# Six spare matmuls in front of the first five products of the second stage of a spectral mixer

## The chip, the cores and the metric

The kernel runs on one core of a Trainium2 chip. The metric is the device time of one execution in microseconds; the median of several executions is compared. A profiled execution gives the trace that is read here.

## The reference

The input `x` has 2048 tokens of 512 channels. It is normalised over the channels, and two branches work on the result: a two-dimensional Fourier filter, and a two-layer network over the token axis, whose output gates the filter's.

```python
xn = _layernorm(x, axis=-1)
# A: filter in the frequency domain
X = rfft2(xn, axes=(-2, -1)) * (w_r + 1j * w_i)
s = irfft2(X, s=(S, D), axes=(-2, -1))
# B: token mixing, W1 is 2048 x 1792, W2 is 1792 x 2048
h = _layernorm(xn, axis=-1)
u = gelu(einsum("bsd,sf->bdf", h, w1) + b1)
y = einsum("bdf,fs->bds", u, w2) + b2
return x + s * silu(y.transpose(0, 2, 1))
```

## The kernel before

Tokens stand on the 128 partitions, 16 of them to a partition, so that there are 16 blocks of 128 tokens by 512 channels. Matrix products that need float32 accuracy are made of three products of operands in the rounded float32 type (`F32R`): high by high, high by low, low by high, where a high part is a copy by ScalarE and a low part a subtraction by VectorE.

The first stage multiplies `w1` with the normalised tokens, in matmuls of 512 columns, and works the forward Fourier transform and the filter in between them. Its last four partial sums are `last_sum` (L759). The results `u` go through GELU and become the moving operands `fa`, `fb`, `fc` and `fd` of the second stage.

The second stage (from L799) works on pairs of token blocks, `p` and `p + 8`, for `p` from 0 to 7. Each pair takes seven products instead of eight, by sums of blocks of `w2` in the manner of Strassen; `ORDER` (L801) is the order of the seven, by their numbers: 1, 2, 5, 6, 3, 7, 4. By the names of their moving operands that is `fd`, `fa`, `fc`, `fc`, `fa`, `fb`, `fb`. The weights of a product are a tile `w2f` with a high and a low half of seven 128x128 blocks each; `w2_forms` (L843) makes them ahead of time, the high half on ScalarE, the low half on VectorE. A product is 21 matmuls of 256 columns, three passes over the seven blocks: the low half is read in the third pass. It accumulates in bank 2 or 3, 4 or 5 of PSUM (`banks`, L903; `products`, L906).

Before the last product of pairs 0 to 6 TensorE works a block of small float32 matmuls, the inverse Fourier transform of the pair (`PARTS`, L44: in pair 0 the even channels, 64x64 matmuls, and the odd ones, 128x128; in pair 1 odd, even and the part over tokens, `spectral`, of 64x512; in pairs 2 to 6 even, `spectral`, odd). In pair 7 `spectral` and `channels` (eight calls of 128x128) stand before the fifth product and a last `spectral` before the seventh. These blocks write banks 6 and 7 of PSUM.

The order on each engine is the order of the program here: an object `Kept` (L131) records every operation as it is called, so that most lines of the trace are L139, the line of that helper. `T` is TensorE, `A` ScalarE, `V` VectorE, `G` GpSimd, `SY` the SyncE queue. A matmul call is a weight load (LDWEIGHTS, engine name PEld) and a matmul (MATMUL, engine name PE) in the trace; the type float32 takes two of each.

`cft` is a float32 constant of 128x130 that is loaded in the first stage (L522).

Of the kernel before, what the change touches and what calls it, by code (L numbers as in the profile page):

```python
# [16 lines left out]
P = 128  # L17
# [124 lines left out]
def spectral_mixer_kernel(tc, x, w1, b1, w2, b2, wk, we, wx, c_f, c_ft, c_d, c_i, c_g, c_h, out):  # L142
    nc = tc.nc
    V, A, G, T, SY = nc.vector, nc.scalar, nc.gpsimd, nc.tensor, nc.sync
# [17 lines left out]
    with tc.tile_pool(name="ps", bufs=1, space=PSUM) as psp, ExitStack() as left, ExitStack() as right:  # L162
        ps = psp.tile([P, 8, 512], F32, name="ps")
        pers = pool(left, "left", "pers", 1)
        cf = pers.tile([P, 64], F32, name="cf")
        cft = pers.tile([P, P + 2], F32, name="cft")
# [158 lines left out]
        def w1_tiles(j):  # L325
            return [[w1r.tile([P, NE1 * P], F32R, name=f"w1{n}{a}_{j}", tag=f"w1{n}{a}", bufs=3) for n in "hl"] for a in range(2)]
# [94 lines left out]
        def form_parts(n, i):  # L421
            t, k = form[i][n]
            return t[:, k, :D // 2], t[:, k, D // 2:]
# [38 lines left out]
        T = Kept(T, keep)  # L462
# [22 lines left out]
        w = w1_tiles(0)  # L485
# [23 lines left out]
        for j in range(NJ):  # L509
# [25 lines left out]
            start, more_stats = j < 3, j + 3 < NJ  # L535
            if more:
                w = w1_tiles(j + 1)
# [248 lines left out]
        for n in range(8):  # L786
            a, b, c, d, e, f = PACE[n]
            u, v, w = ([None] * (k < MADE[n]) for k in range(3))
# [12 lines left out]
        ORDER = (1, 2, 5, 6, 3, 7, 4)  # L801
# [101 lines left out]
        def banks(p):  # L903
            return ps[:, 2 + p % 2, :HD], ps[:, 4, :HD], ps[:, 5, :HD]

        def products(p, n):  # L906

            wf = ready.pop(0)
            bx, by, bz = banks(p)
            o = {1: bx, 6: bx, 7: bx, 4: bx, 2: by, 5: bz, 3: bz}[n]  # L910

            for a, (wi, ui) in enumerate(((0, 0), (0, 1), (1, 0))):
                for m, i in enumerate(FORMS):
                    T.matmul(o, wf[:, wi, i], form_parts(n, i)[ui], start=m + a == 0 and n in (1, 2, 5),
                             stop=m == NH - 1 and a == 2, skip_group_check=n in (6, 3, 7, 4))

        def copied(name, src, where):
            t = where.tile([P, HD], F32, name=name, tag=name.split("_")[0], bufs=1)
            step(A.activation(t, src, AF.Copy))
            return t  # L920

        products(0, ORDER[0])
        p1 = copied("p1_0", banks(0)[0], w2p)
        next(wforms)
# [4 lines left out]
        rest_b = form_b_high(5), form_b_high(6)  # L929
        step(A.activation(e1[:1, 0, :1], b1t[:1, :1], AF.Silu))  # L930
        products(0, ORDER[1])
        next(wforms)
        low_part(rest_b[0])
# [118 lines left out]
        for p in range(NP):  # L1052
# [8 lines left out]
            for k, n in enumerate(ORDER):  # L1061
                started = not p and k < 2
                if not started:
                    products(p, n)
# [81 lines left out]
```

## Time and profile before

| what | value |
| --- | --- |
| median of 3 executions | 365.92 us (365.81 to 365.93) |
| profiled execution | 365.86 us |
| its span, from first to last instruction | 364.1 us |
| TensorE matmuls busy | 357.3 us (98%) |
| TensorE weight loads busy | 308.1 us (85%) |
| VectorE busy | 305.6 us (84%) |
| ScalarE busy | 211.1 us (58%) |
| GpSimd busy | 87.2 us (24%) |

Busy times are those of one profiled execution. Matmuls are pipelined and their printed durations overlap; what a matmul takes in a row of them is read from the distance of starts. In a timeline, neighbours of the same names are one row, with their count behind an x.

### The profile page before, as it was taken

Reading aid. Unit: us, or ns where it says so; the run is one execution under the profiler, and the core shown is the slowest. Engines: PE = TensorE matmul, PEld = TensorE weight load, DVE = VectorE, ACT = ScalarE, POOL = GpSimd, SP = SyncE. Lnnn points to the kernel's source line nnn. Section 1 sums busy time; section 2 is a strip of 40 time slices with the busy share of each in tenths; the row PEclk is TensorE's granted clock in tenths of the full one; section 3 lists DMA queues with packets and bytes.
Section 4 is the critical chain, followed back from the end, with each engine's and each line's share of the span. In section 5 each row is a group of like instructions: output and inputs, shape, how many; then the busy total and the mean of one; then the engine's idle time right before and its main releaser. Section 6 shows DMA issues by size and latency. Waiting matters only on the chain.

```text
span 364.1 us, 8781 instructions
## 1 busy us (share of the span) xinstructions
PE 357.3 (98%) x3444; PEld 308.1 (85%) x3444; DVE 305.6 (84%) x587; ACT 211.1 (58%) x385; POOL 87.2 (24%) x134
## 2 busy tenths in 40 slices
PE   7999999999999999999999999999999999999994
PEld 4788888888877778777888999989898989898983
DVE  5899999967799995999996988687887969696984
ACT  4887788867534426755227875555464546565441
POOL 4233333323222012220120001050403123140330
PEclk9999999999999999999999999999999999999999
DMA  7978899406595686976568388698888989898724
GB/s 208 251 185 200 202 265 311 190 2 164 173 254 193 189 252 165 260 243 200 167 221 181 101 227 180 184 175 204 186 188 209 178 219 167 228 161 220 122 27 90
DMA packets 33293, 68.66 MB, mean 189 GB/s; under 512 B 4612, under 2 KB 19380, under 8 KB 33124
## 3 DMA queue, kind: packets, MB, share of 16 engines
q1 hardware_dynamic: 24276, 42.44, 41.3%
q0 software_dynamic: 8496, 25.01, 32.0%
q10 hardware_dynamic: 480, 0.66, 0.6%
q8 instruction: 27, 0.44, 0.5%
q14 instruction: 14, 0.11, 0.1%
HBM read 59.70 MB, written 8.13 MB: 186 GB/s over the span
## 4 chain that ended last, share of the span: by engine, by line
PE 97%; DMA 1%; ACT 0%; DVE 0%; ACTq 0%; issue 0%; DVEq 0%
PE ps L139 97%; DMA w1r<-in_w_dram 1%; DVE rows L139 0%; ACTq L453 0%; ACT w1h L467 0%; ACT g L139 0%; DVEq L1142 0%
## 5 line engine op out<-in xcount | busy, mean ns | idle before, releaser
L139 PE MATMUL ps<-h,w1h 128*128 128x512 f32 x400 | 116.3, 397 | 0.0
L139 PEld LDWEIGHTS ps<-h,w1h 128*128 128x128 f32 x400 | 72.9, 188 | 19.8 <-issue 4.9
L139 PE MATMUL ps<-h,w1l 128*128 128x512 f32 x200 | 67.6, 390 | 0.0
L139 DVE TENSOR_TENSOR w2f<-a,w2f 128x896 fp32r<-128x896 f32 x36 | 39.2, 1089 | 21.2 <-ACT w2f L139 21.2
L139 ACT ACTIVATE w2f<-a 128x896 fp32r<-128x896 f32 x36 | 36.9, 1025 | 12.9 <-PE ps L139 8.0
L139 PEld LDWEIGHTS ps<-h,w1l 128*128 128x128 f32 x200 | 37.5, 188 | 8.1
L139 PE MATMUL ps<-fb,w2f 128*128 128x256 f32 x336 | 41.9, 279 | 0.0
L139 PE MATMUL ps<-fa,w2f 128*128 128x256 f32 x336 | 41.3, 278 | 0.0
L139 POOL DMA_DIRECT2D s<-in_w_dram x14 | 18.4, 1311 | 95.8 <-DMA s<-in_w_dram 59.8
L139 PEld LDWEIGHTS ps<-fb,w2f 128*128 128x128 f32 x336 | 39.7, 188 | 1.6 <-ACT g L139 0.8
L139 PE MATMUL ps<-fc,w2f 128*128 128x256 f32 x336 | 39.9, 277 | 0.0
L139 PEld LDWEIGHTS ps<-fa,w2f 128*128 128x128 f32 x336 | 39.8, 188 | 0.0
L139 PEld LDWEIGHTS ps<-fc,w2f 128*128 128x128 f32 x336 | 39.2, 188 | 0.0
L155 ACT ACTIVATE w1h<-w1s 128x512 fp32r<-128x512 f32 x26 | 16.2, 632 | 27.0 <-DMA w1s<-in_w_dram 14.7
L139 POOL DMA_DIRECT2D out_dram<-r x28 | 23.6, 1278 | 27.4 <-DVE r L139 27.4
L668 POOL DMA_DIRECT2D xc<-xc x16 | 9.8, 620 | 70.3 <-ACT xc L666 55.1
L308 POOL TENSOR_TENSOR ey<-t 128x256 f32<-128x256 f32 x16 | 15.7, 979 | 43.7 <-DVE t L306 43.7
L139 ACT ACTIVATE w2f<-s 128x896 fp32r<-128x896 f32 x15 | 15.3, 1020 | 14.4 <-PE ps L139 12.5
L470 DVE TENSOR_TENSOR w1l<-w1r,w1h 128x384 fp32r<-128x384 f32 x32 | 21.3, 670 | 0.0
L139 PE MATMUL ps<-fd,w2f 128*128 128x256 f32 x168 | 20.6, 277 | 0.0
L139 ACT ACTIVATE g<-c,b2t 128x256 f32<-128x256 f32 x24 | 12.1, 506 | 14.6 <-DVE c L139 14.6
L268 ACT ACTIVATE h<-x,nbm,rsm 128x256 f32<-128x256 f32 (+1 forms) x34 | 18.4, 593 | 3.7 <-DVE nbm L263 3.3
(135 smaller groups left out, 602.5 us busy)
## 6 DMA issues: line engine op xcount, KB each, us to landing
a<-in_w_dram SPq DMA_DIRECT2D x22, 448.0 KB, 4.3
wt<-in_wk_dram POOLq DMA_DIRECT2D x16, 512.0 KB, 6.2
s<-in_w_dram SPq DMA_DIRECT2D x16, 448.0 KB, 4.6
s<-in_w_dram POOLq DMA_DIRECT2D x16, 448.0 KB, 6.9
w1s<-in_w_dram SPq DMA_DIRECT2D x52, 128.0 KB, 4.4
w1r<-in_w_dram SPq DMA_DIRECT2D x28, 192.0 KB, 5.2
xc<-xc POOLq DMA_DIRECT2D x16, 256.0 KB, 3.1
out_dram<-in_x_dram SPq DMA_DIRECT2D x4, 960.0 KB, 7.4
```

What stands on the lines that cost most here:

```text
L139: return lambda *args, **kw: self.keep(operation(*args, **kw))
L155: return A.activation(hi, src, AF.Copy), V.tensor_sub(lo, src, hi.bitcast(F32))
L268: keep(A.activation(to, v, AF.Identity, bias=m["nb"][:, i], scale=m["rs"][:, i, 1:2]))
L308: G.tensor_add(ey[:, 0::3, :, j], a, b)
L470: keep(V.tensor_sub(dst, src, hi.bitcast(F32)))
L668: keep(G.dma_start(*(v.rearrange("p s t c -> p s (t c)") for v in (there[c::2], here[1 - c::2, ::-1]))))
```

## The change

`products`, which emits the 21 matmuls of one product, first calls a spare if the pair is 0 and there is one for the product's place in the order. A spare is a matmul, or two, of the given weights with the given moving operand, into the first columns of bank 6 of PSUM, where nothing reads it. `w` is the first of the product's own seven high weight blocks, 128x128, of type `F32R`; `cft` is float32. So there are, in front of the five products: one matmul of 2 columns (`F32R`), one of 2 columns (float32), one of 64 columns (`F32R`), two of 2 columns (`F32R`), one of 128 columns (float32).

```diff
@@ -906,6 +906,8 @@
         def products(p, n):
 
             wf = ready.pop(0)
+            if not p and ORDER.index(n) in spares:
+                spares[ORDER.index(n)](wf[:, 0, 0])
             bx, by, bz = banks(p)
             o = {1: bx, 6: bx, 7: bx, 4: bx, 2: by, 5: bz, 3: bz}[n]
 
@@ -913,6 +915,13 @@
+
+        def spare(lhs, rhs, times=1):
+            for _ in range(times):
+                T.matmul(ps[:, 6, :rhs.shape[1]], lhs, rhs, start=True, stop=True)
+
+        spares = {0: lambda w: spare(w, w[:, :2]), 1: lambda w: spare(cft[:, :P], cft[:, :2]), 2: lambda w: spare(w, w[:, :64]),
+                  3: lambda w: spare(w, w[:, :2], 2), 4: lambda w: spare(cft[:, :P], cft[:, :P])}
```

On TensorE, at the border of the two stages: the last matmuls of the first stage (`h`, `w1`), and the first product of pair 0 (`fd`, with the weights `w2f`). The names in brackets are the semaphores that an instruction waits for.

```order
 L139 MATMUL ps<-h_97,w1h_2557 128x512 x2
 L139 MATMUL ps<-h_97,w1l_2558 128x512
+L139 MATMUL ps<-w2f_0_2598 128x2 [waits Activation_49]
 L139 MATMUL ps<-fd_1418,w2f_0_2598 128x256 [waits Activation_49]
 L139 MATMUL ps<-fd_1418,w2f_0_2598 128x256
```

One matmul is new, with a wait of the same kind as the product behind it has; that one's own stays.

On TensorE, between the first product (`fd`) and the second (`fa`) of pair 0:

```order
 L139 MATMUL ps<-fd_2567,w2f_0_2598 128x256 x2
 L139 MATMUL ps<-fd_2656,w2f_0_2598 128x256
+L139 MATMUL ps<-cft 128x2
 L139 MATMUL ps<-fa_1456,w2f_0_2601 128x256
 L139 MATMUL ps<-fa_1563,w2f_0_2601 128x256
```

The float32 spare stands between two products whose own order is as it was. Ahead of the third product the same is done with a matmul of 64 columns, ahead of the fourth with two of 2 columns, and ahead of the fifth with a float32 one of 128 columns. The order on the other four engines is the same before and after.

## Rows read from the trace of the kernel before

**Rows 1.** The page: busy us of each engine, and the chain by engine.

```profile
PE 357.3 (98%) x3444; PEld 308.1 (85%) x3444; DVE 305.6 (84%) x587; ACT 211.1 (58%) x385; POOL 87.2 (24%) x134
...
PE 97%; DMA 1%; ACT 0%; DVE 0%; ACTq 0%; issue 0%; DVEq 0%
```

**Rows 2.** Waits of TensorE: us in total, times, longest us.

```profile
PE ps L139 <- POOL wz L443: 1.1, 1, 1.1
PE ps L139 <- ACT w1h L467: 1.1, 1, 1.1
```

**Rows 3.** Timeline of TensorE, pair 0: start us, us, what, how many.

```profile
202.54 0.39 PE L139 MATMUL ps<-h,w1l 128*128 128x512 f32 x1
202.76 2.63 PE L139 MATMUL ps<-fd,w2f 128*128 128x256 f32 x21
205.24 2.64 PE L139 MATMUL ps<-fa,w2f 128*128 128x256 f32 x21
207.71 5.11 PE L139 MATMUL ps<-fc,w2f 128*128 128x256 f32 x42
212.66 2.64 PE L139 MATMUL ps<-fa,w2f 128*128 128x256 f32 x21
215.13 2.63 PE L139 MATMUL ps<-fb,w2f 128*128 128x256 f32 x21
217.69 1.78 PE L139 MATMUL ps<-cd,yt 64*64 64x64 f32 x40
219.23 2.72 PE L139 MATMUL ps<-fb,w2f 128*128 128x256 f32 x21
221.79 2.63 PE L139 MATMUL ps<-fd,w2f 128*128 128x256 f32 x21
```

**Rows 4.** Timeline of TensorE, pair 1's last product and pair 2.

```profile
239.10 2.74 PE L139 MATMUL ps<-fb,w2f 128*128 128x256 f32 x21
241.68 2.63 PE L139 MATMUL ps<-fd,w2f 128*128 128x256 f32 x21
...
254.05 2.63 PE L139 MATMUL ps<-fb,w2f 128*128 128x256 f32 x21
```

**Rows 5.** Timeline of TensorE, from pair 2's block to pair 3's.

```profile
256.61 0.69 PE L139 MATMUL ps<-cd,yt 64*64 64x64 f32 x32
...
259.01 2.63 PE L139 MATMUL ps<-fb,w2f 128*128 128x256 f32 x21
261.48 2.54 PE L139 MATMUL ps<-fd,w2f 128*128 128x256 f32 x21
263.86 2.54 PE L139 MATMUL ps<-fa,w2f 128*128 128x256 f32 x21
...
273.38 2.54 PE L139 MATMUL ps<-fb,w2f 128*128 128x256 f32 x21
275.85 0.69 PE L139 MATMUL ps<-cd,yt 64*64 64x64 f32 x32
...
280.72 2.54 PE L139 MATMUL ps<-fd,w2f 128*128 128x256 f32 x21
```

**Rows 6.** Weight loads by stretch: stretch, length, busy (count), granted clock, DMA share, GB/s.

```profile
244.15:254.05 9.90, 9.90 (x85) 1.00 0.88 186
261.48:273.38 11.90, 11.90 (x106) 1.00 0.88 170
```

**Rows 7.** Timeline of TensorE, end of pair 7.

```profile
349.07 2.05 PE L139 MATMUL ps<-cd,yt 128*128 128x128 f32 x16
350.88 2.63 PE L139 MATMUL ps<-fa,w2f 128*128 128x256 f32 x21
353.35 2.54 PE L139 MATMUL ps<-fb,w2f 128*128 128x256 f32 x21
355.82 1.09 PE L139 MATMUL ps<-y,cft 64*64 64x512 f32 x8
356.84 2.65 PE L139 MATMUL ps<-fb,w2f 128*128 128x256 f32 x21
```

**Rows 8.** Timeline of the weight loads, pair 7.

```profile
349.07 1.86 PEld L139 LDWEIGHTS ps<-cd,yt 128*128 128x128 f32 x16 [0.81 <-ACT v L139]
350.85 1.33 PEld L139 LDWEIGHTS ps<-fa,w2f 128*128 128x128 f32 x11
```

**Rows 9.** Groups of TensorE by form: busy us, mean ns of one, idle before.

```profile
L139 PE MATMUL ps<-cf,h 64*64 64x64 f32 x512 | 9.3, 221 | 0.0
```

**Rows 10.** Timeline of ScalarE and VectorE: weights of the fifth and sixth product.

```profile
210.48 1.02 ACT L821 ACTIVATE w2f<-a 128x896 fp32r<-128x896 f32 x1 [0.26 <-DVE a L837]
...
211.53 1.09 DVE L825 TENSOR_TENSOR w2f<-a,w2f 128x896 fp32r<-128x896 f32 x1 [0.55 <-ACT w2f L821]
...
213.48 1.08 DVE L139 TENSOR_TENSOR w2f<-s,w2f 128x896 fp32r<-128x896 f32 x1
```

## The prediction

> **What bounds the kernel now.** I read the page's busy times first: TensorE's matmuls fill 357.3 of 364.1 us, no other engine more than 84% (its own weight loads, which overlap, 85%) [rows 1]. Then the chain that ended last, which is TensorE for 97% of the span [rows 1], and TensorE's waits: two, of 1.1 us each, both on the first operands of the program and over by 6.64 us [rows 2]. From there to the last product the matmuls follow one another without a hole, so every matmul that is added lengthens the span by what it takes, and every one that runs faster shortens it. ScalarE, VectorE and the queues matter only if they become late.
>
> The next view is the timeline of TensorE, since the change stands there. The second stage is eight pairs of seven products, each product 21 matmuls of 256 columns in one row of the view (42 where the third and fourth follow each other). A product's length is the distance from its start to the next product's, since the printed durations overlap. In pair 0 that is 2.48 us (202.76 to 205.24) [rows 3]; in pair 3 it is 2.38 us (261.48 to 263.86) [rows 5]. Over five products in a row: 241.68 to 254.05 is 12.37 us for 105 matmuls, 117.8 ns each [rows 4]; 261.48 to 273.38 is 11.90 us for 105, 113.3 ns each [rows 5]. So the same matmuls run at **two paces**, 2.474 and 2.380 us a product, 0.094 us apart. It is not the clock: the granted clock is 1.00, the level of 2.4 GHz, in a stretch of either pace [rows 6]. It is not a wait, as there is none. Within a run of 256-column matmuls the pace never changes; it is set where a run begins. The first run begins behind the 512-column products of the first stage and is slow at once [rows 3]. Behind it nine blocks of small matmuls (the inverse transform's 64x64, 64x512 and 128x128 ones) divide the runs. Three were entered at the slow pace: those of pair 0 and of pair 1 left it slow [rows 3, 4], that of pair 2, at 256.61, made it fast [rows 5]. Six were entered at the fast pace, those of pairs 3 to 6 and two in pair 7, and all left it fast (pair 3 and pair 7 stand in [rows 5, 7]). What in a block decides is in no row: the rows tell that the pace has a memory and that small matmuls can change it.
>
> **The change part by part.** It adds six matmul calls ahead of the first five products of pair 0, and moves nothing else: on the other four engines the order is the same, word for word but for buffer numbers. Slow are 20 products: six of pair 0 up to its block (stretch 0), then its last product and six of pair 1 (stretch 1), then the last of pair 1 and six of pair 2 (stretch 2). At the fast pace they give 0.56, 0.66 and 0.66 us, 1.88 in all. No spare stands in stretch 1 or 2: there the gain comes only if the blocks carry it on.
>
> *What the spares cost.* Each call loads its own 128x128 weights; they are for nothing else. A call of the type float32 is two loads and two matmuls in the records: the block of 16 records at 349.07 is eight calls of the last pair's transform. That block, whose matmuls are shorter than their loads, goes at the loads' pace: 349.07 to 350.85 is 1.78 us for 16, 111 ns each [rows 8]. The spares have 2 to 128 columns, so they too are bound by their loads: four of the rounded type (one, one of 64 columns, two) with one load each, and two of float32 with two each, 8 x 0.111 = **0.89 us**. Below: matmuls with 64x64 weights take 9.3 us for 512 records, 18 ns each [rows 9], which would be 0.15 us for eight; but they load a quarter of the array. Above: the first product behind pair 0's block takes 219.23 to 221.79, 2.56 us, 0.09 more than its neighbours [rows 3]; eight slots at 0.118 and six such re-entries are 1.48 us. I take 0.89, since the block of 128x128 float32 loads is the nearest row. Less than zero it can't be by itself: nothing is removed.
>
> The Trainium skill (TensorE: Matmul & The Clock Gate, section "LDWEIGHTS (loading the stationary operand)") has the load's time go with its columns, P / 1.2, which for 128 is an estimate of 107 ns and a sum of 0.85 us; the rows' 111 ns are near and are used.
>
> *What they wait for, and who waits for them.* Spare 0, 2 and 3 read the high half of the weights that the product behind them reads at once, and two of float32 read a constant that was loaded long before; the first carries the same wait on ScalarE that the first product had. They write bank 6 of PSUM, which the block at 217.69 overwrites and nobody reads in between. The weights are early: the fifth product starts at 212.66 [rows 3] and its high half is written from 210.48 to 211.50, its low half, needed 14 matmuls later, until 212.62 [rows 10]. So no wait is added; delayed by up to 0.9 us, TensorE finds everything ready, and behind it ScalarE and VectorE wait a little longer for PSUM, which costs nothing. If the pace turns fast, TensorE comes at most 0.56 us earlier to the sixth product, whose low half is done by 214.56 [rows 10] and wanted from about 216.8: still early. In pairs 3 to 6 VectorE keeps up with the fast pace already.
>
> *What they may give.* This no row prices: no run of 256-column matmuls in the trace is broken by a single short matmul. By the nearest rows, the blocks, one in three slow entries turned fast and none of six fast ones fell back. The ends are 0 and 1.88 us, or a loss if a block further on that now turns fast stays slow: 0.66 us for each pair that it lasts.
>
> **How it could go.** The profiled execution took 365.86 us for its span of 364.1, and the median of the runs is 365.92; sums below start from the median.
>
> *Forecast: it pays for itself, no more.* Some spares turn the pace, in part of stretch 0 and in one of stretches 1 and 2: 0.28 + 0.66 = 0.94 back for 0.89 spent, **365.9 us**, its own range 365.3 to 366.5. For it: five tries, each at about one in three, and two blocks on the way which the trace never shows entered fast (the other orders of block kept it six times of six).
>
> *Rival: the whole slow stretch turns.* One of the first spares makes the pace fast, the later ones and both blocks keep it: 0.89 - 1.88 = -0.99 at best, -0.75 if half of stretch 0 is lost, 364.9 to 365.2. For it: six of six. Against: it needs all three stretches to come out beyond 0.2%, since two leave 0.89 - 1.32 = -0.43.
>
> *Rival: the pace stays as it is,* and the change only adds its eight loads: 366.81, or 366.4 to 366.7 if products between two spares turn for a while. This is the slower side, with one place, TensorE between 202.76 and 217.69; it decides as soon as pair 0's block is again left slow and pair 1's too, as both are now. For it: these two blocks did so in the trace, and a spare of one matmul is much less than a block of 40.
>
> The Trainium skill (the same page, step 1 of "Step-by-step: what each phase is for") says that loading the next weights does not steal read bandwidth from the running matmul. By that rule alone there is nothing for spares to shift, and it would be this rival; the two paces at one granted clock [rows 4 to 6] speak against the rule as the whole story.
>
> *Rival: a later stretch falls back.* With the pairs shifted, the block at 256.61 that now turns the pace leaves it slow: 0.66 us for each of pairs 3 to 6 concerned on top of 0.89, 367.5 to 369. Against: entered fast this same order of block kept it four times of four.
>
> That the change doesn't do what it says (the spares dropped or merged into one load) is not to be expected, since the program holds all six as matmuls of their own.
>
> **How the numbers follow.** 0.2% of 365.92 is 0.73 us, about what a measurement of this kernel can tell from no change: 365.19 and 366.65 are the limits. That pair 0 ends fast I put between one in three (one try) and 0.87 (five independent tries without a relapse), at 0.6; that a block entered fast stays so, in an order not seen, at 0.65; that one entered slow turns, at 0.3. Both later stretches fast: about 0.33, of which little over half passes 365.19; one: 0.33; none: 0.34, of which half stays under 366.65 by what stretch 0 gives back. In chances: forecast 0.55, whole stretch 0.18, as it is 0.17, fall back 0.10; **faster 0.18, same 0.55, slower 0.27.** The predicted time is the forecast's, 365.9. The range for 8 in 10 takes in the rivals' near ends and the price up to 1.1 us: 365.0 to 367.0.
>
> **What would show it.** In the timeline of TensorE behind the change: six more matmuls between 202.5 and 214 us, and the distances of product starts, 2.47 or 2.38 plus 0.11 a load. A spare works where the distance behind it is 2.38. The block of pair 0 shows by the product at about 219 and by pair 1 whether the pace is carried. Pairs 3 to 6 must stand at 2.38, and TensorE must still have two waits. The prediction is wrong if a load costs far from 0.111 us, if spares cost a re-entry of 0.09 us each, if a third pace turns up, or if the pace changes within a run.

## The result and the profile after

The changed kernel takes 366.69 us (median; the kernel before, beside it, 365.88 us). The ratio is 1.0024, interval 1.0014 to 1.0033: slower by 0.24%, or 0.81 us. The forecast of no change was wrong. What came is the rival "the pace stays as it is", 366.81 us.

The page of after, busy us of each engine, and the waits of TensorE (us in total, times, longest):

```profile
PE 358.9 (98%) x3452; PEld 309.5 (85%) x3452; DVE 305.8 (84%) x587; ACT 211.4 (58%) x385; POOL 87.1 (24%) x134
```

```profile
PE ps L139 <- POOL wz L443: 1.1, 1, 1.1
PE ps L139 <- ACT w1h L467: 0.3, 1, 0.3
```

Eight records are new [rows 1]. There are the same two waits [rows 2], both over by 6.41 us. The second stage begins 0.05 us earlier than before; no wait shows why, and over the kernels of this document its first matmul starts anywhere from 202.57 to 203.00 us. The timeline of TensorE after: pair 0, then the first products of pairs 1, 2 and 3 (start us, us, what, how many):

```profile
202.71 0.17 PE L139 MATMUL ps<-w2f 128*128 128x2 f32 x1
202.74 2.72 PE L139 MATMUL ps<-fd,w2f 128*128 128x256 f32 x21
205.29 0.28 PE L139 MATMUL ps<-cft 128*128 128x2 f32 x2
205.43 2.72 PE L139 MATMUL ps<-fa,w2f 128*128 128x256 f32 x21
207.99 0.19 PE L139 MATMUL ps<-w2f 128*128 128x64 f32 x1
...
210.58 0.28 PE L139 MATMUL ps<-w2f 128*128 128x2 f32 x2
...
213.27 0.38 PE L139 MATMUL ps<-cft 128*128 128x128 f32 x2
213.41 2.72 PE L139 MATMUL ps<-fa,w2f 128*128 128x256 f32 x21
215.97 2.63 PE L139 MATMUL ps<-fb,w2f 128*128 128x256 f32 x21
218.53 1.78 PE L139 MATMUL ps<-cd,yt 64*64 64x64 f32 x40
...
222.63 2.64 PE L139 MATMUL ps<-fd,w2f 128*128 128x256 f32 x21
225.10 2.64 PE L139 MATMUL ps<-fa,w2f 128*128 128x256 f32 x21
...
242.52 2.63 PE L139 MATMUL ps<-fd,w2f 128*128 128x256 f32 x21
245.00 2.63 PE L139 MATMUL ps<-fa,w2f 128*128 128x256 f32 x21
...
262.32 2.54 PE L139 MATMUL ps<-fd,w2f 128*128 128x256 f32 x21
264.70 2.54 PE L139 MATMUL ps<-fa,w2f 128*128 128x256 f32 x21
```

From spare to spare the view gives 2.58, 2.70, 2.59, 2.69 and 2.70 us. A product at the slow pace is 2.474 [rows 3]; so a spare of one load costs 0.11 us, one of two loads 0.22. Their sum: 202.71 to 215.97 is 13.26 us, the same five products before 12.37 (202.76 to 215.13) [rows 3], 0.89 us more. No product behind a spare is faster. Pairs 1 and 2 are slow as before (222.63 to 225.10 and 242.52 to 245.00 are 2.47 and 2.48 us), and pair 2's block turns the pace as before (262.32 to 264.70 is 2.38; [rows 5]). The change pays its price and gets nothing.

### The profile page after: what moved, and what is told of

Same layout as the page of the kernel before. It is cut to its first block, busy times and chain, and to the rows that moved or that the text cites. A ratio compares the mean times of both kernels' runs of the same rounds, so it can differ in the third digit from the quotient of the medians.

```text
span 364.9 us, 8797 instructions
## 1 busy us (share of the span) xinstructions
PE 358.9 (98%) x3452; PEld 309.5 (85%) x3452; DVE 305.8 (84%) x587; ACT 211.4 (58%) x385; POOL 87.1 (24%) x134
## 4 chain that ended last, share of the span: by engine, by line
PE 97%; DMA 1%; DVE 1%; issue 0%; ACT 0%; DVEq 0%
PE ps L139 97%; DMA x<-in_x_dram 1%; DVE rows L139 0%; DVE stm L244 0%; DVE h L272 0%; ACT g L139 0%; DVE tm L229 0%; ACT sdm L223 0%; DVEq L1151 0%; DVE mvm L220 0%; DVE r0m L228 0%; DVE rsm L230 0%; DVE v2m L221 0%; DVE v2m L222 0%
```

## The experiments

Two questions: why does no spare turn the pace, when blocks do, and whose time is the price? Three theories stood at first. LANDING: the place in time, to about a nanosecond, at which a matmul starts decides. BLOCK: only blocks of other shapes can turn the pace. CHANCE, that of the prediction: every disturbance has some chance. All kernels below start from the kernel before, but for e7. In a table of spares the key is (pair, place of the product in the order), the value the columns of weights and of the moving operand; `w` is the first half of the product's weight tile, which gives the spare its weights and its moving operand, `c` the constant `cft`, and `P` is 128. The results of these spares go to banks 2 to 5 of PSUM instead of 6 and are overwritten; e7 keeps bank 6. Three dots in a fence stand for lines left out. Where no ratio is given, a time is that of one execution, and the reading rests on distances within its trace.

**e1_wide.**

```diff
+            if (p, ORDER.index(n)) in spares:
+                for kind, cols, wide in spares[p, ORDER.index(n)]:
+                    spare(p, wf, kind, cols, wide)
...
+        spares = {(0, 0): [("w", P, 258)], (0, 1): [("w", P, 260)], (0, 2): [("w", P, 262)], (0, 3): [("w", P, 264)], (0, 4): [("w", P, 266)], (0, 5): [("w", P, 268)], (1, 2): [("w", P, 270)], (1, 3): [("w", P, 272)], (1, 4): [("w", P, 274)], (1, 5): [("w", P, 276)], (2, 2): [("w", P, 256)], (2, 3): [("w", P, 320)], (2, 4): [("w", P, 384)], (2, 5): [("w", P, 512)]}
```

> One spare matmul of the product's own first weights in front of 14 of the slow products, each of another width, all at least as wide as a product's matmul: 258, 260, 262, 264, 266, 268 columns in front of the first six products of pair 0, 270, 272, 274, 276 in front of products three to six of pair 1, and 256, 320, 384, 512 in front of products three to six of pair 2. A product behind a spare that works takes 2.38 us, otherwise 2.47. Theory LANDING: the pace is decided by where, to about a nanosecond, the first matmuls of a run land against something that goes on its own in the engine; the change's spares are shorter than their own weight load, so all of them put the next product at the same place whatever their width, and none of these places is one that gives the fast pace. A spare wider than 256 columns moves the place by 0.4 ns a column, so some widths turn the pace and some do not: at least one and not all of the 14. Theory BLOCK: only a block of many small matmuls of other shapes can change the pace; none of the 14 does, and the time is the one before plus 4142 columns at 2.4 GHz, 1.73 us, and some 0.1 us for entries: 367.7 us. Theory CHANCE, that of the prediction: every spare has about one chance in three and a fast run stays fast: almost all products behind the second or third are fast, whatever the width, and the two blocks keep it: 366.0 to 366.3 us.

Measured: 367.43 us. Timeline of TensorE, the third to fifth product of pair 0:

```profile
207.94 0.28 PE L139 MATMUL ps<-w2f 128*128 128x262 f32 x1
208.06 2.63 PE L139 MATMUL ps<-fc,w2f 128*128 128x256 f32 x21
210.53 0.29 PE L139 MATMUL ps<-w2f 128*128 128x264 f32 x1
210.67 2.54 PE L139 MATMUL ps<-fc,w2f 128*128 128x256 f32 x21
213.04 0.29 PE L139 MATMUL ps<-w2f 128*128 128x266 f32 x1
```

Behind 262 columns a product takes 208.06 to 210.53, 2.47 us; behind 264, 210.67 to 213.04, 2.37. Five of 14 widths gave a fast product: 264, 268, 270, 274 and 512. And 266, 272 and 276 columns, each entered at the fast pace, made it slow again. BLOCK falls, since a single matmul turns the pace; CHANCE falls, since the fast pace does not stay. Pair 0's block was entered fast here and left it slow.

The records of the starts, in nanoseconds, say more. The 512-column matmuls of the first stage start every 226.67 ns, which is 34 x 6.67. At the fast pace a matmul takes 113.3 ns, 17 x 6.67; at the slow pace three take 353.3 ns, 53 x 6.67. Taken modulo 6.67 ns, called the beat here, and counted from the 512-column matmuls of the same trace, the starts at the fast pace lie within a nanosecond of zero; those at the slow pace go through three places in turn, **A** (about 5.3 to 6.0 ns), **B** (2.7 to 3.7) and **C** (1.0 to 2.0). The records are in whole nanoseconds, so a place is known to about one. (The "parts" of an expectation below are 0.83 ns, an eighth of the beat.) Since 21 is a multiple of three, each product at the slow pace starts at the same place as the one before it. By the place at which the spare started:

| place | left slow | made fast |
| --- | --- | --- |
| A | 260, 262 | 274 |
| B | 384 | 268, 270, 512 |
| C | 256, 320 | 264 |

Not in the table are 258 columns, which started at A directly behind the first stage and left it slow, and the three that were entered fast. The start of the product behind does not decide by itself: behind 262 columns its first two starts lay at 0.3 and 6.6 ns, just as behind 512, but the third came 122 ns later instead of 113, and it was slow. So what the table holds is the place, the width and the outcome, not a reason.

**e2_short_loads.**

```diff
+        spares = {(0, 0): [("w", 32, 2)], (0, 1): [("w", 64, 2)], (0, 2): [("w", 96, 2)], (0, 3): [("w", 64, 2)], (0, 4): [("w", 32, 2)], (0, 5): [("w", 96, 2)], (1, 2): [("w", 64, 64)], (1, 3): [("w", 32, 128)], (1, 4): [("w", 64, 256)], (1, 5): [("w", 32, 256)]}
```

> Spares whose weights are only 32, 64 or 96 columns of the product's first block: in front of the first six products of pair 0 with 32, 64, 96, 64, 32, 96 columns of weights and 2 moving columns; in front of products three to six of pair 1 with 64 by 64, 32 by 128, 64 by 256 and 32 by 256 (weights by moving). Theory LANDING: a shorter load, and a moving operand near or past it, puts the next product at another place than a load of 128 columns; some of the ten turn the pace, not all. Theory BLOCK: none. Theory CHANCE: as in the run with wide spares, all from the second or third on. Price: a load of 128 columns was 0.11 us in the trace; with fewer columns between 0.03 us and that, so 0.3 to 0.8 us for the eight short ones and about 0.1 each for the two of 256: if nothing turns 366.4 to 366.9 us.

Measured: 366.86 us, no product turned. LANDING had expected some, and missed: none of these loads and widths changed the pace, the two of 256 columns included. Nor does a spare's own load matter to the price: pair 0 up to its block took 15.60 us (202.62 to 218.22), 14.93 before [rows 3], 0.112 us for each of six spares, whether 32, 64 or 96 columns were loaded.

```profile
202.62 0.17 PE L139 MATMUL ps<-w2f 128*32 128x2 f32 x1
...
218.22 1.78 PE L139 MATMUL ps<-cd,yt 64*64 64x64 f32 x40
```

**e4_spares_in_fast.**

```diff
+        spares = {(3, 2): [("w", P, 2)], (3, 3): [("c", P, 2)], (3, 4): [("w", P, 64)], (3, 5): [("w", P, 2)] * 2, (3, 6): [("c", P, P)]}
```

> The change's five kinds of spares, but in pair 3, which runs at the fast pace: in front of its products three to seven stand one of 2 columns, one of 2 columns of float32, one of 64 columns, two of 2 columns, one of 128 columns of float32. All are shorter than their loads. Theory LANDING: they put the next product at the one place that gave the slow pace in the changed kernel, since a load of 128 columns sets that place by itself: the products behind them go at 2.47 us until the next block, 0.3 to 0.5 us are lost on top of the price of 0.89 us, 367.1 to 367.3 us. Theory BLOCK and theory CHANCE (a fast run has never been seen to fall back): the products stay at 2.38 us, only the price is paid, 366.8 us.

Measured: 368.45 us. Timeline of TensorE, pair 3, then behind pair 4's block:

```profile
261.49 2.54 PE L139 MATMUL ps<-fd,w2f 128*128 128x256 f32 x21
263.87 2.54 PE L139 MATMUL ps<-fa,w2f 128*128 128x256 f32 x21
266.25 0.17 PE L139 MATMUL ps<-w2f 128*128 128x2 f32 x1
266.28 2.72 PE L139 MATMUL ps<-fc,w2f 128*128 128x256 f32 x21
268.84 0.28 PE L139 MATMUL ps<-cft 128*128 128x2 f32 x2
...
301.98 2.63 PE L139 MATMUL ps<-fd,w2f 128*128 128x256 f32 x21
304.46 2.63 PE L139 MATMUL ps<-fa,w2f 128*128 128x256 f32 x21
```

The product ahead of the first spare takes 2.38 us; the next, with its spare, 2.59, which is the slow 2.474 and 0.11. So the first of the change's spares doesn't merely fail to turn a run fast, it turns a fast one slow. From there to pair 5's block all 18 products are slow, at 0.094 us each; with the price of 0.89 that makes 2.58, and 2.63 was measured. CHANCE and BLOCK fall here; LANDING's sum was short because it let the next block mend the pace.

**e3_block_order.**

```diff
-PARTS = ("EO", "OES", *["ESO"] * 5, "SF")
+PARTS = ("EO", "ESO", *["ESO"] * 5, "SF")
```

> No spare at all; the block of pair 1 runs in the order of pairs 2 to 6 (even channels, the part over tokens, odd channels) instead of odd, even, tokens. Theory BLOCK (the order of a block's parts decides, and the even, tokens, odd order turns a slow entry fast, as at 256.61 us): the last product of pair 1 and the first six of pair 2 go at 113.3 ns a matmul, 0.66 us are saved, 365.2 us. Theory LANDING: the block's inner order sets where the next product lands relative to the block's own last matmuls, so it may turn as well, and the distances inside the block must then be those of pair 2's block. Theory CHANCE (a block turns one slow entry in three, whatever its order): more likely no change, 365.9 us.

Measured: 366.03 us; the block of pair 1, in the order that turned pair 2's, left the pace slow. So the order alone does not decide. By the records of all runs, the place of the last matmul ahead of a block in this order does: entered fast, it stayed fast each time; entered at B it turned fast, ten times of ten (before, after, e2, e3, e4 twice, e6, e7, e11, e12); at A it stayed slow, four of four (e3, e4, e6, e12), and the next block was then entered at B. Pair 0's block, even and odd, behaves otherwise: in all 14 kernels that have it in this order it left the pace slow, from each of the three places and also in the four that entered it fast (e1, e5, e7, e13).

**e5_chosen_widths and e6_other_widths.** Widths chosen from the table of places, for the second product of pair 0 (A) and the first of pair 1 (B); and the same kernel with two other widths.

```diff
-PARTS = ("EO", "OES", *["ESO"] * 5, "SF")
+PARTS = ("EO", *["ESO"] * 6, "SF")
...
+        spares = {(0, 1): [(P, 274)], (1, 0): [(P, 270)]}
```

```diff
-        spares = {(0, 1): [(P, 274)], (1, 0): [(P, 270)]}
+        spares = {(0, 1): [(P, 260)], (1, 0): [(P, 384)]}
```

> Two spares whose widths are chosen by where the earlier wide spares landed, and pair 1's block in the order even, tokens, odd: one of 274 columns in front of the second product of pair 0, one of 270 columns in front of the first product of pair 1. Theory LANDING: in a slow run the starts of the matmuls, taken modulo 6.67 ns, stand at three places that repeat, and every product of a run starts at the same one; from the place of the second product of pair 0 a spare of 274 columns made a run fast, from the place of the first of pair 1 one of 270 did. So products two to six of pair 0 go fast (5 x 0.094 = 0.47 us), its block loses it again, as it did behind the spare of 268 columns; all seven products of pair 1 and, since a block in the order of pairs 2 to 6 that is entered fast has kept it each time, six of pair 2 go fast (13 x 0.094 = 1.22 us); the two spares cost 0.25 us: 1.44 us less than before, 364.4 us. Theory CHANCE: each try one in three, as independent tries: likely nothing or one stretch, 365.0 to 366.1 us. Theory BLOCK: no change of pace, 366.1 us.

> The same kernel as the one with chosen widths, but for the two widths: 260 columns instead of 274, 384 instead of 270. Theory LANDING: from these places 260 and 384 columns left a run slow, so both stretches stay slow and the price of 0.12 and 0.17 us is paid; the block of pair 1 in its new order is entered slow and leaves it slow as it did without spares: 366.1 us (0.66 us less if it should land otherwise). Theory CHANCE: the width is nothing to it, so the same as the kernel with chosen widths, whatever that gives.

Measured: 364.40 us, ratio 0.9961, interval 0.9947 to 0.9975; and 366.16 us. Timeline of TensorE with the chosen widths:

```profile
205.11 0.29 PE L139 MATMUL ps<-w2f 128*128 128x274 f32 x1
205.24 2.54 PE L139 MATMUL ps<-fa,w2f 128*128 128x256 f32 x21
207.62 4.92 PE L139 MATMUL ps<-fc,w2f 128*128 128x256 f32 x42
...
221.33 0.29 PE L139 MATMUL ps<-w2f 128*128 128x270 f32 x1
221.45 2.55 PE L139 MATMUL ps<-fd,w2f 128*128 128x256 f32 x21
223.84 2.54 PE L139 MATMUL ps<-fa,w2f 128*128 128x256 f32 x21
...
240.70 2.54 PE L139 MATMUL ps<-fd,w2f 128*128 128x256 f32 x21
243.08 2.54 PE L139 MATMUL ps<-fa,w2f 128*128 128x256 f32 x21
```

And with the other widths:

```profile
205.27 2.64 PE L139 MATMUL ps<-fa,w2f 128*128 128x256 f32 x21
207.74 5.11 PE L139 MATMUL ps<-fc,w2f 128*128 128x256 f32 x42
...
221.99 2.63 PE L139 MATMUL ps<-fd,w2f 128*128 128x256 f32 x21
224.47 2.63 PE L139 MATMUL ps<-fa,w2f 128*128 128x256 f32 x21
```

The chosen widths both turned the pace (205.24 to 207.62 and 221.45 to 223.84, 2.38 and 2.39 us), pair 1's block kept it (240.70 to 243.08); the other two did not (205.27 to 207.74 and 221.99 to 224.47, 2.47 and 2.48 us). Both times came out as LANDING gave them, 364.4 and 366.1. Two numbers in the source are worth 1.8 us.

**e7_change_one_wide.** From the changed kernel:

```diff
-4: lambda w: spare(cft[:, :P], cft[:, :P])
+4: lambda w: spare(w[:, :P], w[:, :270])
```

> The changed kernel with one of its spares replaced: the last one, in front of the fifth product of pair 0, is one matmul of 270 columns of the product's own first weights instead of the float32 one of 128 columns. Theory LANDING: the fifth product starts behind two spares of 2 columns at the place from which 270 columns made a run fast twice over; products five and six go at 2.38 us (0.19 us), the spare costs 0.12 instead of 0.23 us, the block behind leaves the run slow: 0.3 us less than the changed kernel, 366.4 us. Theory BLOCK: only the price falls, 366.55 us, and both products stay at 2.47 us.

Measured: 366.54 us in one run. In the timeline the fifth product goes at the fast pace, and the sixth too:

```profile
213.50 2.55 PE L139 MATMUL ps<-fa,w2f 128*128 128x256 f32 x21
215.89 2.54 PE L139 MATMUL ps<-fb,w2f 128*128 128x256 f32 x21
```

From the first spare to the block it is 15.54 us (202.82 to 218.36), in the changed kernel 15.82 (202.71 to 218.53): 0.28 less, as LANDING gave it. In the median 0.15 is seen, since TensorE came to the second stage 0.11 us later. So one spare of the change, made wider than a product's matmul, does what five groups of short ones don't.

**e8_whose_load.**

```diff
+        spares = {(0, 0): [(32, 2)] * 2, (0, 1): [(P, 2)] * 2, (0, 2): [(32, 2)] * 2, (0, 3): [(P, 2)] * 2, (0, 4): [(32, 2)] * 4, (0, 5): [(P, 2)] * 4}
```

> Short spares of 2 columns in rows of two and four, in front of the six products of pair 0: two with 32 columns of weights, two with 128, two with 32, two with 128, four with 32, four with 128. It asks whose load the price of a short spare is. Theory NEXT LOAD: a short spare has its own load hidden behind the product before it, and uncovers the load of whatever follows; a row of n spares uncovers n - 1 spares' loads and the product's, of 128 columns. So a row of two with 32 columns costs 0.11 us and a short load (0.03 to 0.06 us), 0.14 to 0.17; of two with 128 columns 0.22; of four with 32 columns 0.2 to 0.3; of four with 128 columns 0.45 us. Theory PER CALL, that of the prediction read literally: every spare costs 0.11 us whatever it loads: 0.22, 0.22, 0.22, 0.22, 0.45, 0.45 us. In sum 367.3 us by the first and 367.6 us by the second. No product's pace turns by theory LANDING.

Measured: 366.77 us. Timeline of TensorE:

```profile
202.93 0.20 PE L139 MATMUL ps<-w2f 128*32 128x2 f32 x2
...
205.55 0.28 PE L139 MATMUL ps<-w2f 128*128 128x2 f32 x2
...
208.25 0.20 PE L139 MATMUL ps<-w2f 128*32 128x2 f32 x2
...
213.56 0.26 PE L139 MATMUL ps<-w2f 128*32 128x2 f32 x4
...
216.24 0.50 PE L139 MATMUL ps<-w2f 128*128 128x2 f32 x4
```

Less 2.474 us for the product, two spares of 32 columns cost 0.15 us (202.93 to 205.55), two of 128 columns 0.23 (205.55 to 208.25), four of 32 columns 0.21 (213.56 to 216.24). That is NEXT LOAD: a short spare's own load lies under the matmul ahead of it; what it uncovers is the load of whatever follows, 0.11 us for 128 columns, some 0.03 for 32. The time was 0.53 us under the expected 367.3: pair 1's block, entered at C instead of A, left the pace fast, which was not foreseen and gives seven products at 0.094, 0.66 us; the second stage began 0.17 us later than before (202.93 against 202.76).

**e9_widened_second and e10_widened_first.** No spare; the first matmul of a product is itself made wider.

```diff
+                    if m + a == 0 and (p, ORDER.index(n)) in wider:
+                        (t, k), cols = form[i][n], wider[p, ORDER.index(n)]
+                        T.matmul(ps[:, {1: 2 + p % 2, 2: 4, 5: 5}[n], :cols], wf[:, wi, i], t[:, k, :cols], start=True, stop=False)
+                        continue
...
+        wider = {(0, 1): 274, (1, 0): 270}
```

(in e10 `{(0, 0): 274, (1, 0): 270}`; pair 1's block as in e5)

> No spare: the first matmul of the second product of pair 0 is made 274 columns wide instead of 256, that of the first product of pair 1 270 columns (the moving operand runs on into the low half that stands behind the high one; the 18 and 14 columns more go to a part of the bank that nobody reads), and pair 1's block has the order even, tokens, odd. Theory LANDING: what turned the pace behind the chosen spares is the width of one matmul in a row of others of 256, whatever it computes, so the same stretches go fast, and instead of two spares of 0.12 us only 18 and 14 columns are paid, 0.01 us in all: 364.4 less 0.23 is 364.2 us. Theory CHANCE or a theory by which an extra matmul or weight load is needed: the pace stays, 365.9 us.

> As the kernel with the second product widened, but it is the first product of pair 0, behind the 512-column matmuls of the first stage, whose first matmul has 274 columns. Theory LANDING: the first matmul of that product starts within a nanosecond of the same place of the beat as the second product's did, so all six products are fast, 0.09 us more are saved: 364.1 us. If the place behind the 512-column matmuls is another, pair 0 stays slow up to its block (0.47 us lost against the kernel with the second product widened, 364.65 us) and only pairs 1 and 2 are fast.

Measured: 369.21 us, ratio 1.0097 (1.0080 to 1.0115), and 369.10 us, ratio 1.0090 (1.0077 to 1.0103). A clear miss, by 5 us. Timeline of e9 behind pair 2's block:

```profile
261.56 2.64 PE L139 MATMUL ps<-fd,w2f 128*128 128x256 f32 x21
264.04 2.64 PE L139 MATMUL ps<-fa,w2f 128*128 128x256 f32 x21
```

The widened matmuls turned nothing, and now pair 2's block does not either, nor any behind it: the whole second stage is slow (261.56 to 264.04 is 2.48; [rows 5] have 2.38). By the records each of these blocks is entered at C and left so that the next is entered at C again, twelve of twelve in the two kernels. In this order a block entered at C never mended the pace.

Why did the same widths miss? The starts in nanoseconds, last matmul of the first product, the 274-column matmul, and what follows (e13, below, is e5 with other weights in its spares):

```
e5   204992 205110 205236 205351 205464 205577   distances 118 126 115 113 113
e13  205117 205235 205360 205475 205589 205702   distances 118 125 115 114 113
e9   205106 205224 205349 205466 205584 205701   distances 118 125 117 118 117
```

Behind the wide matmul the next start comes after 125 or 126 ns in all three; e13 and e9 even stand at the same places up to there. Only the one after it differs, 115 ns where the pace turned and 117 where it did not. So the records of the starts do not show what made the difference, and the two next kernels ask for it.

**e12_own_operand and e13_own_weights.** e5 again, whose spares read the weight tile as their moving operand. e12 lets them read what the widened matmuls read; e13 changes their weights alone.

```diff
-            T.matmul(bank[:cols, :wide], flat[:, :cols], flat[:, :wide], start=True, stop=True)
+            T.matmul(bank[:, :wide], wf[:, 0, FORMS[0]], t[:, k, :wide], start=True, stop=True)
```

```diff
-            T.matmul(bank[:cols, :wide], flat[:, :cols], flat[:, :wide], start=True, stop=True)
+            T.matmul(bank[:, :wide], wf[:, 0, FORMS[0]], flat[:, :wide], start=True, stop=True)
```

> The kernel with chosen widths, but each of its two spares reads what the product behind it reads first, its own moving operand, 274 and 270 columns of it, and its own first weights, instead of the weight tile by its first block. So a spare does exactly what the widened matmuls did that left the pace slow, but it is an extra matmul. Theory WIDTH ALONE: the width and the place decide, the widened matmuls missed because they were not an extra matmul: fast as with the chosen widths, 364.4 us. Theory OPERAND TOO: what a matmul reads shifts its end by a nanosecond as its width does; with the operands of the widened kernel it misses as that one did: both stretches stay slow, 366.1 us, and up to 369.4 us if the blocks of pairs 1 to 6 are then entered at the place from which they never turn.

> The kernel with chosen widths, with only the weights of the two spares changed: the block that the product behind uses first, instead of the first block of the tile; the moving operand stays the weight tile. Theory WIDTH ALONE: 364.4 us. Theory OPERAND TOO, by the moving operand: 364.4 us as well, and the run with the product's own moving operand misses; by the weights: this run misses too, 366.1 to 369.4 us.

Measured: 366.13 us and 364.44 us. Timeline of TensorE of e12, where the view puts the spare and its product into one row, since their names are the same:

```profile
205.17 2.76 PE L139 MATMUL ps<-fa,w2f 128*128 128x274 f32 x22
207.77 5.11 PE L139 MATMUL ps<-fc,w2f 128*128 128x256 f32 x42
```

From 205.17 to 207.77 is 2.60 us, 0.125 for the spare and the slow 2.474. That is OPERAND TOO, by the moving operand. From place A, 274 columns of the weight tile gave the fast pace in all three kernels that had them there (e1, e5, e13), 274 columns of `fa` in neither of two (e9, e12). From B it was 270 columns of the tile four times of four (e1, e5, e7, e13), 270 of `fd` in neither of two (e9, e10); but there the 270 columns were the product's own first matmul and not an extra one, so that for this width the operand is not separated from that. In e12 the first spare's miss changed the place of the second, so that one compares with nothing.

**e11_free_order and e14_free_and_264.** No spare but other block orders, and the same with one spare at a product that starts at C.

```diff
-PARTS = ("EO", "OES", *["ESO"] * 5, "SF")
+PARTS = ("OE", *["ESO"] * 6, "SF")
```

```diff
+        spares = {(1, 0): [(P, 264)]}
```

> No spare and no wider matmul: only the orders of two blocks, odd and even instead of even and odd in pair 0, and even, tokens, odd in pair 1. Theory LANDING: another last part of the block puts the next product at another place, by luck the one that makes it fast (then 0.66 us are saved in pair 1 and, as the block of pair 1 is then entered fast, 0.66 us in pair 2: 364.6 us), or not: 365.9 us. Theory CHANCE gives the fast case one in three. What must hold by theory LANDING in either case: the start of the second matmul behind the block stands within a nanosecond of the beat's one place in the fast case and not in the slow one.

> The two changed block orders without a spare (365.02 us in one run: pair 1's block is entered at the place from which pair 2's block turned fast before, and it turned), and one spare of 264 columns in front of the first product of pair 1. Theory LANDING: that product starts at the place of the beat (2.4 of 8 parts) from which 264 columns made a run fast once. Its six products go fast (0.56 us) for a spare of 0.13 us, and the block behind it is entered fast and keeps it: 364.6 us. If it misses, the spare moves the place at which the block of pair 1 is entered: 365.1 us if that block turns all the same, 365.8 to 366.0 us if it does not and the one behind it does, up to 369 us if none does.

Measured: 365.02 us in one run, and 364.87 us, ratio 0.9971 (0.9960 to 0.9983). In e11 pair 0's block left the pace slow, but at a place from which pair 1's was entered at B, and that one turned: between the two cases expected, at no cost. What LANDING said must hold did not separate the cases: the second matmul behind pair 0's block stood 0.8 ns from the fast place, within the nanosecond allowed, and the pace was slow. In e5, behind the same pair's block in the old order, it stood 0.1 ns from it and was slow too. In e14 the spare of 264 columns turned pair 1 as its place said:

```profile
221.66 0.29 PE L139 MATMUL ps<-w2f 128*128 128x264 f32 x1
221.80 2.54 PE L139 MATMUL ps<-fd,w2f 128*128 128x256 f32 x21
224.18 2.54 PE L139 MATMUL ps<-fa,w2f 128*128 128x256 f32 x21
```

The median is 0.27 us over the 364.6 worked out, with the mechanism as forecast; the one profiled execution took 364.65. The fastest kernel is e5, 1.4 us under the kernel before and 2.3 under the changed one.

So LANDING holds as a table: what one place, width and operand gave, they gave again in e5, e6, e7, e13 and e14. As a reason, that the start of a matmul alone decides, it is not shown, and e1, e9 and e11 speak against it.

## Why the prediction was wrong

*What bounds the kernel* held: no hole on TensorE, two waits, and every addition shows in the end time.

*The price* of 0.89 us came out as 0.89 us. The wording was not right: the load that costs is not the spare's own but the next one's, which the spare is too short to cover (e2, e8). In the change both have 128 columns, so the number is the same. The Trainium skill (TensorE: Matmul & The Clock Gate, section "LDWEIGHTS (loading the stationary operand)") has a load go with its columns; by it 32 columns are an estimate of 27 ns. The four spares of 32 columns come near it: 0.206 us less 0.112 for the product's load, over three, is 31 ns.

*What they may give* is the step that failed: the 0.94 us that the forecast counts back came out as nothing. "By the nearest rows, the blocks, one in three slow entries turned fast" was carried over to five spares as five tries, and the six of six for entries at the fast pace was carried over to the blocks of pairs 0 and 1, whose order the trace had never shown entered fast. The runs show neither. Of 28 products behind spares shorter than the load that follows them (after, e2, e4, e7, e8), 28 were slow, one of them directly behind a product at the fast pace. Nor were the blocks' three entries draws: what a block does goes with its order and the place at which it is entered. And pair 0's block, put at 0.65 to carry the fast pace on, lost it four times of four (e1, e5, e7, e13): even where a spare does turn pair 0, the gain ends at its block. Why short spares never turn the pace is not shown. LANDING has them all put the next product at one place, but the products behind those of e2 started all over the beat (0.3, 3.3, 0.6, 6.6, 2.9 and 0.3 ns).

*The rivals.* "The pace stays as it is" came, at 366.81 predicted and 366.69 measured; 0.05 of the difference is the earlier start. What stood for it, that a single matmul is much less than a block, is not the reason, as e1 shows. The rule of the Trainium skill named with it (same page, step 1 of "Step-by-step: what each phase is for"), by which loading the next weights doesn't take from the running matmul's reads, gave this time. No run here tests that rule; with the loads left alone, the width and the source of one moving operand decide over the pace (e6, e12), of which it says nothing. "A later stretch falls back" didn't come, but it can: e9 and e10 lost 0.66 us, seven products at 0.094, in each pair from 3 on, 3.4 us in all with pair 7, which the rival left out. The changed kernel was spared since its six spares happened to leave the place at which pair 2's block is entered at B.

*The chances.* The 0.55 on no change rested on the misread step, and slower had half of that.

What stays open: what in the engine keeps the beat of 6.67 ns, why a moving operand from another tile gives another pace, and why short spares give none. The runs show that these matter, not why.

## What to carry to other kernels

Where runs of equal matmuls go at two paces under one granted clock and without a wait, look at the starts modulo a common beat before calling it chance: the trace's records show the place, and a table of what was tried from which place forecast 364.4 us to a tenth. The same table missed by 5 us when the operand changed with the width kept (e9, e10). A matmul put in as a nudge and shorter than the weight load behind it costs that load and never made a run fast here (28 of 28); being longer was not enough either (e2, e6). And a pace won this way hangs on nanoseconds: a block's order or an operand's tile moved this kernel between 1.4 us less and 3.4 us more, so compare two versions of such a kernel by stretches in the trace, not by the total alone.

## What was not expected of the hardware

- Weight load and 256-column matmul pairs settle into one of two locked patterns, 113.3 ns or three in 353.3 ns, at the same granted clock [rows 6].
- One spare of 274 columns, read from the weight tile, turned a run of 105 matmuls by 4.5 ns each (e5); one of 260 columns didn't (e6), nor one of 274 from another tile (e12).
- A block of small matmuls acts by its order and the place of its entry: even, tokens, odd kept the fast pace each time, gave it from B (10 of 10) and left it slow from A (4 of 4) and C (12 of 12); even, odd left it slow from everywhere (14 of 14).
- The slow pattern can sustain itself through the blocks: e9, with every block from pair 1 on entered at C, is slow to its end and takes 3.4 us more than the kernel before.
- A 2-column matmul costs 0.112 us whatever it loads, between 32 and 128 columns, if a load of 128 columns follows.
